# Reordering the row loads, crossbar transposes and value loads of each batch in a fused attention and feed-forward kernel

## Chip, cores, metric

One core of a Trainium2 chip. The metric is the time of the whole program on the device in microseconds (us); quoted times are medians of all runs of a kernel. Runs marked slow, more than 1.5% above the fastest of the same kernel, are left out of ratios. A ratio is the mean time of one kernel's fast runs over the mean of the other's of the same rounds on the same chip, so it is not quite the ratio of the medians.

## The reference

Attention over a band of 16 positions on each side plus block summaries (maximum of 32 keys, mean of 32 values), then a feed-forward layer with a scaled swish.

```python
# q, k, v: (4 batches, 8 heads, 768, 64) float32;  w_in (512, 2048), w_out (2048, 512)
k_sum = k.reshape(B, H, 24, 32, D).max(axis=3)
v_sum = v.reshape(B, H, 24, 32, D).mean(axis=3)
scores_l = scale * q @ k.T ;  masked to |i - j| < 16
scores_s = scale * q @ k_sum.T + log(32)
a = softmax(concat(scores_l, scores_s))
x = a @ concat(v, v_sum)                    # then (B*S, 512)
h = x @ w_in
out = (h * sigmoid(beta * h)) @ w_out       # (3072, 512) float32
```

## The kernel before

Eight blocks of 384 rows (4 batches, 2 halves each) are worked through. Block i has an h phase (16 tiles of `x @ w_in`, Silu) and an o phase (`@ w_out`); beside the o phase PE also makes the scores and the attention of block i+1. Side work is put at numbered positions of the two phases: `side_h`, position p, stands ahead of h tile p; `side_o`, position p, stands ahead of o part p (12 parts of 4 matmuls). Each engine's instructions are issued in the order in which they are written.

Three kinds of transfer serve the next batch. GpSimd (POOL) issues loads that change float32 to bf16: key rows, query rows, and values in two halves ("even" and "odd" tiles). SP issues crossbar transposes of the loaded key rows (`k_bar`, four a batch), of query rows (`q_bar`, one a block) and of half of the attention result x (`x_dma`, one a block), and the stores of the output. `hold(src)` is a one-element copy on POOL: nothing behind it on POOL is issued before `src` is there.

```python
def k_bar(b, g):                                        # SP
    nc.sync.dma_start_transpose(out=kT_bufs[i][:, W:W + S]..., in_=krow[(b, g // 2)]...)
def q_bar(b, c):                                        # SP
    nc.sync.dma_start_transpose(out=t..., in_=qrow.pop((b, c))...)
def x_dma(b, g, c):                                     # SP
    nc.sync.dma_start_transpose(out=x_tile(b, c)[:, g:g + 2]..., in_=xp[(b, g // 2, c)]...)
def q_fill(b, g, c): ...                                # DVE: qTT -> q2, two copies a pair
def hold(src):                                          # POOL
    nc.gpsimd.tensor_copy(out=tick[:], in_=src)
# ... in block i = (b, c):
        elif b + 1 < B:
            hold(xT[(b, c)][0:1, npair - 1, 0:1])
            if c == 0:
                for g in PAIRS:
                    load_k_rows(b + 1, g)
                load_q_rows(b + 1, 0)
                load_v6(b + 1)
                load_v_even(b + 1)
            else:
                load_v_odd(b + 1)
                load_q_rows(b + 1, 1)
# ...
            elif c == 0:
                    for g in PAIRS:
                        add(side_o, 7 + g, k_bar, b + 1, g)
# ...
            if nxt > 2:
                add(side_h, 0, q_bar, b2, c2)           # (b2, c2): the next block
                for g in PAIRS:
                    add(side_h, 10 + g, q_fill, b2, g, c2)
            for g in PAIRS:
                add(side_o, (-1, 0, 3, 4)[g], scores, b2, g, c2)
# ...           # x of the next block: pairs 0 and 1 by x_dma at side_o 5.1,
                # pairs 2 and 3 on PE (x_pe) at side_o 9
```

The softmax here doesn't subtract the row's maximum and nothing guards it: scores larger than these inputs give would overflow.

## Time and profile before

| | before |
|---|---|
| time, median of 2 runs | 246.98 us (246.56 to 247.40) |
| span of the profiled run | 243.7 us |
| PE busy | 223.5 us (92%) |
| mean granted PE clock | 0.97 |

PE (the matmul engine, TensorE) sets the pace, so the table is read for what it lacks: 20 us in which PE stands still, and some time in which it is busy at a lower clock. (The granted clock is the share of its full clock that PE was given, as the trace records it.) Which lines show where that is comes with the prediction below.

### The profile page before, as it was taken

To read this page: it belongs to the slowest core of one execution; us is meant where nothing else is said; L and a number is where in the kernel's file an instruction comes from. 1 tells how busy PE (TensorE), PEld (TensorE's weight loads), DVE (VectorE), ACT (ScalarE), POOL (GpSimd) and SP (SyncE) were. 2 spreads that over 40 slices of the span, in tenths; PEclk is the share of its full clock that TensorE was granted. 3 is DMA by queue.
4 is the path that set the end of the run, shared out by engine and by line. 5 is a ranking of instruction groups with operands and counts; after the bars stand their busy time and mean duration, and the time that the engine had idled before them with its cause. 6 is when DMAs were issued, how large, how long until landed. Compare 5 with 4: busy or idle time off the path is not lost.

```text
span 243.7 us, 4675 instructions
## 1 busy us (share of the span) xinstructions
PE 223.5 (92%) x1871; PEld 122.0 (50%) x1871; DVE 118.5 (49%) x337; ACT 152.4 (63%) x246; POOL 68.3 (28%) x106
## 2 busy tenths in 40 slices
PE   6969799979999999999769999999669999999993
PEld 2544456445555565555335555555334456556541
DVE  7564797958945504635386504634384613520000
ACT  2766379537767489648735489657725389939610
POOL 7649491560000396034000396044000000000000
PEclk9997999999999999999979999999968999999999
DMA  7999999999701399999931299999931340121012
GB/s 129 181 179 178 203 195 193 200 146 167 119 0 46 78 167 137 145 189 124 172 20 46 76 168 138 159 175 130 165 19 45 79 108 3 43 78 43 0 43 86
DMA packets 100565, 27.86 MB, mean 114 GB/s; under 512 B 89392, under 2 KB 97600, under 8 KB 100544
## 3 DMA queue, kind: packets, MB, share of 16 engines
q0 software_dynamic: 71664, 14.98, 77.6%
q1 hardware_dynamic: 28736, 12.46, 25.0%
q8 instruction: 14, 0.23, 0.4%
q10 hardware_dynamic: 144, 0.13, 0.2%
q14 instruction: 7, 0.06, 0.1%
HBM read 31.52 MB, written 6.29 MB: 155 GB/s over the span
## 4 chain that ended last, share of the span: by engine, by line
PE 68%; DMA 14%; DVE 8%; ACT 5%; issue 2%; POOL 1%; SPq 0%; ACTq 0%; DVEq 0%; POOLq 0%
PE o_ps L472 33%; PE h_ps L454 23%; DMA qTT<-qrow 13%; PE s_ps L329 4%; PE av_ps L355 3%; DMA qnat<-in_q_dram 2%; DVE w_out_sb L442 2%; DVE q L271 1%; PE px L372 1%; DVE v L397 1%; PE vm_ps L390 1%; ACT h_sb L462 1%; DVE x_nat L359 1%; DVE km L239 1%; DVE q L298 1%
## 5 line engine op out<-in xcount | busy, mean ns | idle before, releaser
L472 PE MATMUL o_ps<-w_out_sb,h_sb 128*128 128x512 bf16 x384 | 94.5, 389 | 0.0
L454 PE MATMUL h_ps<-xT,w_in_sb 128*128 128x384 bf16 x512 | 86.7, 326 | 1.1 <-ACT h_sb L462 0.8
L462 ACT ACTIVATE h_sb<-h_ps,beta_sb 128x384 bf16<-128x384 f32 x128 | 73.9, 581 | 18.6 <-PE h_ps L454 11.1
L454 PEld LDWEIGHTS <-w_in_sb 128*128 128x128 bf16 x512 | 49.2, 98 | 35.5 <-issue 3.0
L472 PEld LDWEIGHTS <-h_sb 128*128 128x128 bf16 x384 | 35.7, 100 | 35.9 <-issue 3.6
L331 ACT ACTIVATE attn<-s_ps 128x768 bf16<-128x768 f32 x28 | 22.2, 811 | 14.8 <-PE s_ps L329 14.7
L271 DVE COPY q<-qTT 64x384 bf16<-64x384 bf16 x40 | 13.9, 347 | 35.4 <-DMA qTT<-qrow 34.8
L484 ACT COPY o_sb<-o_ps 128x512 f32<-128x512 f32 x23 | 13.5, 586 | 27.5 <-PE o_ps L472 24.9
L334 DVE TENSOR_TENSOR attn<-attn,mask 128x768 bf16<-128x768 bf16 x28 | 15.5, 558 | 21.8 <-ACT attn L331 21.1
L490 POOL COPY tick<-xT 1x1 bf16<-1x1 bf16 x4 | 0.7, 178 | 76.2 <-ACT xT L373 76.2
L329 PE MATMUL s_ps<-q,kw 128*128 128x128 bf16 x168 | 14.5, 231 | 8.2 <-DVE q L271 8.1
L329 PEld LDWEIGHTS <-kw 128*128 128x128 bf16 x168 | 12.2, 103 | 13.3 <-issue 9.3
L359 DVE TENSOR_TENSOR x_nat<-av_ps,r 128x384 bf16<-128x384 f32 x32 | 17.8, 558 | 1.1
L257 DVE TENSOR_REDUCE km<-kT 128x24 bf16<-128x768 bf16 x8 | 7.6, 950 | 17.7 <-DMA kT<-krow 17.7
L373 ACT COPY xT<-px 128x384 bf16<-128x384 bf16 x19 | 9.1, 479 | 10.7 <-PE px L372 10.5
L100 POOL DMA_DIRECT2D qrow<-in_q_dram x15 | 13.4, 914 | 2.0 <-DMA krow<-in_k_dram 2.0
L95 POOL DMA_DIRECT2D krow<-in_k_dram x16 | 13.1, 852 | 0.9 <-issue 0.9
L355 PEld LDWEIGHTS <-attn 128*64 128x64 bf16 x384 | 8.0, 111 | 9.5 <-issue 5.5
L397 DVE COPY v<-vm 32x1536 bf16<-32x1536 bf16 (+1 forms) x20 | 10.9, 558 | 3.6 <-ACT vm L393 2.7
L479 DVE COPY o_sb<-o_ps 128x256 f32<-128x256 f32 x1 | 0.4, 424 | 24.3 <-PE o_ps L472 24.3
L157 ACT ACT_TABLE_LOAD x9 | 11.5, 1283 | 0.9 <-PEq L705 0.8
L247 DVE COPY kw<-kT 128x288 bf16<-128x288 bf16 x56 | 12.0, 268 | 0.0
(96 smaller groups left out, 182.3 us busy)
## 6 DMA issues: line engine op xcount, KB each, us to landing
out_dram<-o_sb SPq DMA_DIRECT2D x23, 256.0 KB, 3.0
v<-in_v_dram POOLq DMA_DIRECT2D x3, 768.0 KB, 10.4
w_in_sb<-in_moe_w_in_dram POOLq DMA_DIRECT2D x4, 512.0 KB, 6.8
w_out_sb<-in_moe_w_out_dram POOLq DMA_DIRECT2D x4, 512.0 KB, 15.9
qrow<-in_q_dram POOLq DMA_DIRECT2D x15, 128.0 KB, 11.8
krow<-in_k_dram POOLq DMA_DIRECT2D x16, 96.0 KB, 6.7
vs<-in_v_dram SPq DMA_DIRECT2D x3, 384.0 KB, 6.2
v<-in_v_dram POOLq DMA_DIRECT2D x2, 576.0 KB, 12.7
```

The costliest lines, as they stand in the source:

```text
L100: nc.gpsimd.dma_start(out=qrow[(b, c)][:, m], in_=q_r2[b, c, :, m])
L271: nc.vector.tensor_copy(out=q2[r, :, hh].rearrange("p (m t) f -> p m t f", t=2), in_=t[r])
L329: nc.tensor.matmul(big[:, j // 3, j % 3 * P:(j % 3 + 1) * P], kw[:, j, :], q2[:, j].rearrange("p h q -> p (h q)"), start=True, stop=True)
L331: nc.scalar.activation(out=a.rearrange("p (k n) -> p k n", k=2), in_=big[:, :, 0:CT], func=ACTF.Exp, scale=scale)
L334: nc.vector.tensor_mul(out=av4, in0=av4, in1=mask[:, c * TC:(c + 1) * TC, None, :].to_broadcast([P, TC, 2, QT]))
L355: nc.tensor.matmul(ov[r, j // 2, hh], av4[:, j, hh], vr[:, hh, c * TC + j, 0:D + 1], start=True, stop=True)
L359: nc.vector.tensor_mul(out=x, in0=ov[:, :, :, 0:D], in1=r[:, :, :, None].to_broadcast([P, CC, 2, D]))
L397: nc.vector.tensor_copy(out=v_rows(b, g)[KR:P, :, t0:t1, 0:D], in_=vm[KR:P, 2 * i:2 * i + 2, None].to_broadcast([P - KR, 2, t1 - t0, D]))
L454: nc.tensor.matmul(h_ps[(i, ni)][:, 0:CT], w_in_sb[:, ki, ni * P:(ni + 1) * P], x[:, ki], start=(ki == 0), stop=(ki == k1 - 1))
L462: nc.scalar.activation(out=h_sb[i][:, ni], in_=hp[:, 0:CT], func=ACTF.Silu, scale=beta_sb[:, ni:ni + 1])
L472: nc.tensor.matmul(o_ps[ms][:], h_sb[i][:, ni, ms * P:(ms + 1) * P], w_out_sb[:, ni, :], start=(ni == 0), stop=(ni == k2 - 1))
L484: nc.scalar.copy(out=o_sb[:], in_=o_ps[ms][:])
```

## The change

Its intent: bring a new batch's keys and queries first, transpose them as they land (in the h phase, where PE needs nothing from the SP queue), and let the values come only after the last key transpose.

```diff
         elif b + 1 < B:
-            hold(xT[(b, c)][0:1, npair - 1, 0:1])
             if c == 0:
+                hold(xT[(b, c)][0:1, npair - 1, 0:1])
                 for g in PAIRS:
                     load_k_rows(b + 1, g)
                 load_q_rows(b + 1, 0)
                 load_v6(b + 1)
-                load_v_even(b + 1)
             else:
-                load_v_odd(b + 1)
                 load_q_rows(b + 1, 1)
 ...
                     for g in PAIRS:
-                        add(side_o, 7 + g, k_bar, b + 1, g)
+                        add(side_h, 14, k_bar, b + 1, g)
+                    add(side_h, 14, q_bar, b + 1, 0)
+
+                    def v_next(b=b):
+                        hold(kT_bufs[(b + 1) % 2 * npair + npair - 1][0:1, W:W + 1])
+                        load_v_even(b + 1)
+                        load_v_odd(b + 1)
+
+                    add(side_h, 14, v_next)
 ...
-                at_v = 13.5 if i == 1 else 10
+                at_v = 14
 ...
-                add(side_h, at_v, vsum)
+                if i == 1:
+                    add(side_o, 0.5, vsum)
+                else:
+                    add(side_h, at_v, vsum)
                 for g in PAIRS:
-                    add(side_h, at_v + 1 + g, ... v_spread ...)
+                    add(side_o, 1 + g * .5, ... v_spread ...)
             if nxt > 2:
-                add(side_h, 0, q_bar, b2, c2)
 ...
+            if c and b + 1 < B:
+                add(side_o, 8.5, q_bar, *divmod(i + 2, NC))
 ...
             def v1():
-                hold(w_out_sb[0:1, k2 * 3 // 4 - 1, 0:1])
+                hold(w_out_sb[0:1, k2 - 1, 0:1])
 ...
-            add(side_o, 3.2, v1)
+            add(side_o, 5.7, v1)
```

## The prediction

> **What bounds the kernel now.** I read the page's first parts, then cut the span into stages, then the waits of each stage, then the order of time around the waits. Eight blocks of rows are worked through; a stage here is one block's h phase (64 matmuls of w_in, with Silu) followed by its o phase (48 matmuls of w_out, with the scores and the attention of the next block).
>
> ```profile
> PE 223.5 (92%) x1871; PEld 122.0 (50%) x1871; DVE 118.5 (49%) x337; ACT 152.4 (63%) x246; POOL 68.3 (28%) x106
> PE 68%; DMA 14%; DVE 8%; ACT 5%; issue 2%; POOL 1%; SPq 0%; ACTq 0%; DVEq 0%; POOLq 0%
> ```
>
> PE is busy 92% of 243.7 us, so a gain comes only from its 20.2 us of idle and from time in which it is busy at a lower clock. The DMA share of the chain is no 14% to win: the chain runs back through the query transpose while PE works beside it. What counts is how late that transpose ends. The stages tell it (columns: stretch, length, then busy us and instructions of PE, PEld, DVE, ACT, POOL, then granted clock, DMA share, GB/s):
>
> ```profile
> 83.90:107.80 23.90, 23.82 (x192) 13.44 (x190) 7.75 (x20) 17.83 (x28) 11.98 (x15) 1.00 1.95 154
> 107.80:138.90 31.10, 27.19 (x200) 14.74 (x198) 17.99 (x53) 17.93 (x28) 4.95 (x6) 0.95 0.93 92
> 138.90:162.50 23.60, 23.60 (x192) 13.37 (x190) 7.75 (x20) 17.82 (x28) 12.01 (x15) 1.00 1.85 157
> 162.50:195.30 32.80, 28.61 (x199) 15.00 (x198) 17.79 (x53) 17.93 (x28) 4.79 (x5) 0.90 0.88 87
> 195.30:218.90 23.60, 23.60 (x192) 13.39 (x190) 7.75 (x20) 17.82 (x28) 0.00 (x0) 1.00 0.23 60
> ```
>
> These are blocks 2 to 6. Blocks 2, 4 and 6 take 23.6 to 23.9 us with no PE idle. Blocks 3 and 5, which prepare a new batch, take 31.1 and 32.8 at clocks of 0.95 and 0.90. Their waits (first block 3, then block 5; the columns are us in total, times, longest):
>
> ```profile
> PE s_ps L329 <- DVE q L271: 3.9, 2, 3.4
> DVE q L271 <- DMA qTT<-qrow: 3.5, 1, 3.5
> ```
> ```profile
> PE s_ps L329 <- DVE q L271: 4.2, 2, 3.7
> DVE q L271 <- DMA qTT<-qrow: 2.9, 1, 2.9
> ```
>
> So PE stands still because the new batch's queries reach it late. In block 5, second by second, the clock is seen to fall after that:
>
> ```profile
> 177.00:178.00 1.00, 0.00 (x0) 0.00 (x0) 0.36 (x2) 0.00 (x0) 0.00 (x0) 1.00 1.17 71
> 178.00:179.00 1.00, 0.62 (x6) 0.61 (x6) 0.95 (x3) 0.00 (x0) 0.00 (x0) 0.54 0.00 0
> 183.00:184.00 1.00, 1.00 (x4) 0.29 (x2) 0.91 (x2) 0.00 (x0) 0.00 (x0) 0.50 0.00 0
> 185.00:186.00 1.00, 1.00 (x11) 0.65 (x10) 0.00 (x0) 0.30 (x1) 0.00 (x0) 1.00 0.00 0
> ```
>
> Why are the queries late? On the SP queue (in order), the four key transposes of batch 2 stand behind block 2's output store and x transpose; the first goes out at 103.97, and the query transpose behind them at 111.26. By then the odd half of the values (issued at 107.71) and the next query rows (from 109.48) are in flight too, and it lands 11.5 us later, at 122.8. The five query transposes landed in 8.1, 11.5, 7.7, 11.4 and, the last one, with no loads beside it, 3.7 us.
>
> A second, smaller site is block 0's o phase. The row is start, length, what:
>
> ```profile
> 47.21 3.06 DVE L442 TENSOR_SCALAR w_out_sb<-w_out_sb,inv_beta 128x512 bf16<-128x512 bf16 x4
> 51.03 0.34 PE L372 MATMUL px<-identity,x_nat 128*128 128x128 bf16 x3 [1.60 <-DVE x_nat L359]
> ```
>
> Four scalings of w_out take 3.06 us here, while four took 1.14 from 44.18; the longest is 1,627 ns where the median of all sixteen is 347. At that time POOL is issuing the value loads of batch 1 (45.88 to 49.9), and PE then waits 1.60 us for x_nat, which stands behind the scalings.
>
> **What the Trainium skill says.** First, "TensorE: Matmul & The Clock Gate", section "Part 1: The HAM clock gate": the array drops to half clock after about one idle window of 3.4 us, and needs about 3.4 us of sustained work to come back. The trace agrees: waits whose longest pieces are 3.4 and 3.7 us are followed by clocks of 0.50, for about 3.5 us in block 3 (123.4 to 126.9) and 7 us in block 5 (177.9 to 184.9). Second, "SBUF — State Buffer", section "Who interferes with whom": a tensor_scalar in a two-port mode and a GpSimd operation exclude one another for a whole instruction, and the descriptors of DMAs issued from GpSimd are written through that port. The 1,627 ns beside POOL's issues fits; the trace shows the coincidence, not the port. Third, "DMA: Bandwidth & Descriptors", section "Queues, rings and completion order": each DMA engine goes round its queues packet by packet, so a transpose on the SP queue shares with loads on the GpSimd queue. The 3.7 us alone against 11.5 beside loads agrees.
>
> **The change part by part.** PE's instruction count does not change (3,743 rows in both orders); DVE's 40 query copies, 8 maxima and 56 key copies stay, as do all loads and transposes. It is an exchange of order.
>
> (a) Block 2 (and 4): the four key transposes and the first query transpose go ahead of the o phase's store and x transpose on SP, so they go as the rows land. The key loads are issued from 83.65 to 90.1, and landed in 3.0 to 7.4 us (median 6.7). Each key transpose occupies the engines about 1.25 us (four landed between about 104.5 and 109.5), and slows the loads it cuts into. I estimate the last key transpose lands at 96 to 98, the query rows at 96 to 98, and the query transpose, beside the value load, 8 us later: 104 to 106, in place of 122.8. The queries are first needed in block 3 near 118, so the wait goes, with 12 us to spare.
>
> (b) The values are held until that last key transpose: even half issued near 97 instead of 94.6, odd half behind it instead of at 107.7. At the 10.4 and 12.7 us to landing of these loads, shortened for the odd half because it follows in one queue, I expect 108 to 110 and 114 to 117. The value sum on PE moves to h tile 14 of block 3 (about 117), the attention matmuls that read the odd half come at about 128. Both hold.
>
> (c) The second query transpose (for the batch's second half) moves from the start of the even block to the o phase before it, before the key loads. It ends near 86 instead of 93.5; it cost PE 0.08 us, so this wins nothing by itself, but it leaves the engines free for the key loads.
>
> (d) Block 1's value sum and spreads move into its o phase. PE work is the same 1.63 us (1.41 + 0.22); the spreads (1.97 us DVE) sit before attention, where DVE waited for ACT 1.44 and 0.50 us anyway. About 0.
>
> (e) Block 0: value loads wait for the last scaling. DVE saves 3.06 − 1.14 = 1.92 us; PE waits 1.60 of it. Take 1.6. The loads move some 3 us later, and the value sum that needs them moves later too.
>
> The sum: block 3 without waits should be an even block plus its value sum, 23.6 + 1.63 = 25.2 us. Gain 31.1 − 25.2 = 5.9 in block 3, 32.8 − 25.2 = 7.6 in block 5. This holds the pure stall (3.9 and 4.2) and the half-clock time (1.5 and 3.3: half of 3.0 and 6.5 busy us at 0.50, which adds to 5.4 and 7.5, so the two counts agree). With (e): 5.9 + 7.6 + 1.6 = 15.1 us. Against this I put 1 us for each of the two batches for the rival below: 247.0 − 15.1 + 2.0 = 233.9, called 234.
>
> **The rivals.** First: the wait moves to the x transpose. Before, it was issued at 102.64 and landed in 3.7 us, at 106.3, and block 3's first h matmul ran at 107.89, so it has 1.5 us of slack. Afterwards it stands on SP behind a query transpose that runs beside both halves of the values and the next query rows, with no pause at 104.5 to 110 as now. SP was held 3.8 us by one such transpose. If SP is held until 103, or the x transpose takes 8 us like its larger relative, block 3 starts 1 to 4 us late. Against it: at 102.64 the even values were in flight too, and it took 3.7. A wait under 3.4 us should not cost the clock, so this would take back 2 to 6 us in all: 236 to 239. I give it 30%, and 1 us a batch on average.
>
> Second: the total of transfers binds. Then something merely comes late elsewhere, at (b). Before, DMA worked from 83.6 to about 123 of a 55 us cycle (two stages) with a hole near 110, so there is room; if the odd values came after 128, up to 3 us a batch would come back: 237 to 240. 7%.
>
> Third: the transpose lateness is hidden and the stall has another cause, such as DVE's work before the query copies. DVE sat idle 3.5 us just before the first of them, so I give it 3%; the time would be about 245.
>
> Fourth: the clock does not recover because some new short waits add up to an idle window. Then 3 to 5 us of the gain are lost: 237 to 239. 7%.
>
> **Range and chances.** With no rival, 231.9 to 232.5; with a small x wait, 234; with the first rival at full strength, 238. So 230.5 to 238.5 for 8 in 10. The threshold for faster by 2% is 242.0, which needs 5 of the 15 us; only the third rival, or two others together, miss it. Faster 0.95, same 0.04, slower 0.01.
>
> **What would show it.** Right: in blocks 3 and 5 the wait of scores for the query copies is under 0.3 us, the granted clock is 1.00, and both stages take 25 to 26 us; key transposes lie between 87 and 98; the scalings are all near 350 ns and PE's 1.60 us wait is gone. Wrong at (a) or the first rival: PE waits for the x transpose at the start of blocks 3 and 5. Wrong at (b): the value sum or the attention waits for a value load. It would be wrong altogether if the key transposes, beside their own loads, took so long that the hold kept the values past 117.

## The result

| | before | after |
|---|---|---|
| time, median of 2 runs | 246.98 us | 237.03 us (236.59 to 237.48) |
| ratio of fast runs | | 0.9597 (95%: 0.9492 to 0.9703) |
| span of the profiled run | 243.7 us | 235.8 us |
| mean granted PE clock | 0.97 | 0.985 |

Two later groups on other chips gave the changed kernel a ratio of 0.9582 and of 0.9645. It is faster by 3.6 to 4.2%; its medians in the three groups (237.03, 236.39 and 238.50 us) lie 2.4 to 4.5 us above the 234 us that I had said.

From the page of the kernel before, the chain of work that ended last; then the page of the changed kernel. In the chain, the query transpose (qTT) has gone and the x transpose (xT) has come:

```profile
PE o_ps L472 33%; PE h_ps L454 23%; DMA qTT<-qrow 13%; PE s_ps L329 4%; PE av_ps L355 3%; DMA qnat<-in_q_dram 2%; DVE w_out_sb L442 2%; DVE q L271 1%; PE px L372 1%; DVE v L397 1%; PE vm_ps L390 1%; ACT h_sb L462 1%; DVE x_nat L359 1%; DVE km L239 1%; DVE q L298 1%
```
```profile
PE 221.7 (94%) x1871; PEld 121.2 (51%) x1871; DVE 116.7 (50%) x337; ACT 152.0 (64%) x246; POOL 67.9 (29%) x106
PE h_ps L454 36%; PE o_ps L472 32%; DMA xT<-x_nat 5%; PE s_ps L329 4%; PE av_ps L355 4%; PE vm_ps L390 3%; DMA qnat<-in_q_dram 2%; PE px L372 1%; PE vm_ps L166 1%; DVE km L239 1%; POOL knat L81 1%; DVE q L298 1%; ACT q L298 1%; POOL qnat L8
```

The stages of blocks 2 to 6 of the changed kernel, with the columns of the same table in the prediction:

```profile
83.12:106.94 23.82, 23.81 (x191) 13.29 (x189) 11.17 (x29) 17.80 (x28) 15.53 (x18) 1.00 1.74 148
106.94:134.02 27.08, 25.44 (x197) 13.91 (x198) 14.34 (x45) 17.81 (x28) 1.10 (x3) 1.00 1.17 113
134.02:157.85 23.83, 23.82 (x191) 13.29 (x189) 11.17 (x27) 17.80 (x28) 14.96 (x17) 1.00 1.53 147
157.85:187.18 29.33, 27.13 (x198) 14.51 (x199) 15.23 (x48) 17.80 (x28) 1.95 (x3) 0.94 1.26 101
187.18:210.83 23.65, 23.65 (x192) 13.38 (x191) 7.74 (x20) 17.80 (x28) 0.00 (x0) 1.00 0.21 54
```

Blocks 3 and 5 went from 31.1 and 32.8 us to 27.1 and 29.3; an even block plus its value sum would be 25.2. What holds them now is at their start. The timeline of PE, with the wait and its releaser in brackets:

```profile
108.58 9.27 PE L454 MATMUL h_ps<-xT,w_in_sb 128*128 128x384 bf16 x56 [1.64 <-DMA xT<-x_nat]
160.05 10.95 PE L454 MATMUL h_ps<-xT,w_in_sb 128*128 128x384 bf16 x56 [2.21 <-DMA xT<-x_nat]
```

The wait for the queries is gone, and a wait for x has come. The same 56 matmuls take 9.27 us in block 3 and 10.95 in block 5, and the windows of block 5, microsecond by microsecond, say why: the granted clock (third column from the end) falls after the wait.

```profile
159.00:160.00 1.00, 0.00 (x0) 0.00 (x0) 1.00 (x5) 0.00 (x0) 0.80 (x1) 1.00 2.29 166
161.00:162.00 1.00, 1.00 (x5) 0.50 (x4) 0.95 (x5) 0.58 (x1) 0.00 (x0) 0.50 2.42 155
164.00:165.00 1.00, 1.00 (x8) 0.59 (x7) 0.00 (x0) 0.73 (x2) 0.00 (x0) 1.00 2.47 158
```

Around block 2's x transpose the SP queue stands like this (start, length of the issue, what), with the query transpose and a store shortly ahead of x; the key transposes, not shown, were issued from 87.33 to 95.1:

```profile
99.88 1.27 SPq L262 DMA_TRANSPOSE qTT<-qrow  x1
101.25 0.98 SPq L485 DMA_DIRECT2D out_dram<-o_sb  x1
102.33 1.26 SPq L378 DMA_TRANSPOSE xT<-x_nat  x1
```

and POOL lets the values go just then, when the last key transpose has landed:

```profile
100.44 0.18 POOL L490 COPY tick<-kT 1x1 bf16<-1x1 bf16 x1 [7.94 <-DMA kT<-krow]
100.96 2.23 POOL L414 DMA_DIRECT2D v<-in_v_dram  x1 [0.34 <-issue]
```

x landed 6.2 us after its issue in block 2 and 6.5 in block 4 (3.7 and 3.0 before).

In block 0 the scalings are quick again (DVE's timeline), and PE's wait of 1.60 us became 0.57 us, now for a copy on ACT:

```profile
47.39 1.13 DVE L442 TENSOR_SCALAR w_out_sb<-w_out_sb,inv_beta 128x512 bf16<-128x512 bf16 x4
```

From the first scores matmul of block 0's o phase to the end of the last wait (59.43 before, 58.55 after) it takes 19.4 us where it took 20.4. Block 1, to which part (d) belongs, takes 24.57 us in both.

### The profile page after: what moved, and what is told of

Its sections match the earlier page's. It is cut to its first block, busy times and chain, and to the rows that moved or that the text cites. A ratio compares the mean times of both kernels' runs of the same rounds, so it can differ in the third digit from the quotient of the medians.

```text
span 235.8 us, 4672 instructions
## 1 busy us (share of the span) xinstructions
PE 221.7 (94%) x1871; PEld 121.2 (51%) x1871; DVE 116.7 (50%) x337; ACT 152.0 (64%) x246; POOL 67.9 (29%) x106
## 3 DMA queue, kind: packets, MB, share of 16 engines
q1 hardware_dynamic: 28736, 12.46, 25.2%
## 4 chain that ended last, share of the span: by engine, by line
PE 82%; DMA 7%; DVE 3%; ACT 2%; POOL 2%; issue 1%; DVEq 0%; POOLq 0%
PE h_ps L454 36%; PE o_ps L472 32%; DMA xT<-x_nat 5%; PE s_ps L329 4%; PE av_ps L355 4%; PE vm_ps L390 3%; DMA qnat<-in_q_dram 2%; PE px L372 1%; PE vm_ps L166 1%; DVE km L239 1%; POOL knat L81 1%; DVE q L298 1%; ACT q L298 1%; POOL qnat L84 1%; DVE v L397 0%
## 5 line engine op out<-in xcount | busy, mean ns | idle before, releaser
L454 PE MATMUL h_ps<-xT,w_in_sb 128*128 128x384 bf16 x512 | 88.3, 330 | 4.9 <-DMA xT<-x_nat 3.9
L472 PE MATMUL o_ps<-w_out_sb,h_sb 128*128 128x512 bf16 x384 | 91.7, 379 | 0.0
L454 PEld LDWEIGHTS <-w_in_sb 128*128 128x128 bf16 x512 | 49.7, 99 | 40.6 <-DMA xT<-x_nat 4.8
L472 PEld LDWEIGHTS <-h_sb 128*128 128x128 bf16 x384 | 34.7, 98 | 34.0 <-issue 0.4
L484 ACT COPY o_sb<-o_ps 128x512 f32<-128x512 f32 x23 | 13.4, 585 | 27.6 <-PE o_ps L472 25.0
L247 DVE COPY kw<-kT 128x288 bf16<-128x288 bf16 x56 | 14.1, 331 | 0.0
L100 POOL DMA_DIRECT2D qrow<-in_q_dram x15 | 13.4, 934 | 0.0
L329 PEld LDWEIGHTS <-kw 128*128 128x128 bf16 x168 | 11.1, 98 | 4.2
L329 PE MATMUL s_ps<-q,kw 128*128 128x128 bf16 x168 | 12.8, 219 | 0.0
L355 PE MATMUL av_ps<-v,attn 128*64 128x65 bf16 x384 | 10.1, 199 | 1.2 <-DVE v L397 1.1
```

The source lines that it names most:

```text
L100: nc.gpsimd.dma_start(out=qrow[(b, c)][:, m], in_=q_r2[b, c, :, m])
L247: nc.vector.tensor_copy(out=kw[:, t::2, 0:KR], in_=src)
L329: nc.tensor.matmul(big[:, j // 3, j % 3 * P:(j % 3 + 1) * P], kw[:, j, :], q2[:, j].rearrange("p h q -> p (h q)"), start=True, stop=True)
L355: nc.tensor.matmul(ov[r, j // 2, hh], av4[:, j, hh], vr[:, hh, c * TC + j, 0:D + 1], start=True, stop=True)
L454: nc.tensor.matmul(h_ps[(i, ni)][:, 0:CT], w_in_sb[:, ki, ni * P:(ni + 1) * P], x[:, ki], start=(ki == 0), stop=(ki == k1 - 1))
L472: nc.tensor.matmul(o_ps[ms][:], h_sb[i][:, ni, ms * P:(ms + 1) * P], w_out_sb[:, ni, :], start=(ni == 0), stop=(ni == k2 - 1))
```

## The experiments

The edits are against the changed kernel, but for the two that start from the kernel before. The table is the overview; ratios are to the kernel before in the same rounds.

| run | edit | median us | ratio (95%) | PE waits for x, blocks 3 and 5, us |
|---|---|---|---|---|
| after_again | none | 236.39 | 0.9582 (0.949 to 0.967) | 2.19, 2.06 |
| x_on_pe | x of blocks 2, 4 on PE | 232.36 | 0.9456 (0.939 to 0.952) | none |
| x_before_q | x ahead of the query transpose | 232.21 | 0.9442 (0.939 to 0.950) | none |
| v_after_x | values held until x | 231.38 | 0.9429 (0.935 to 0.950) | none |
| keep_busy | dummy matmuls in the wait | 236.59 | 0.9599 (0.954 to 0.965) | 0.41, 0.91 behind 1.73 of dummies |
| only_late_v1 | before, part (e) alone | 244.88 | 0.9904 (0.984 to 0.997) | none |
| only_k_early | before, early transposes alone | 251.17 | 1.0147 (1.007 to 1.022) | 7.39, 7.66 |
| v_not_held | no hold on the values | 248.83 | 1.0095 (1.004 to 1.015) | 6.34, 6.58 |
| not_held_x_first | no hold, x first | 243.75 | 0.9993 (0.990 to 1.009) | 3.33, 3.40 |
| q_late_again | part (c) undone | 233.69 | 0.9572 (0.948 to 0.966) | 1.12, none |
| after_pair | none | 238.50 | 0.9645 (0.958 to 0.971) | 2.20, 3.32 |
| q_late_pair | part (c) undone | 234.50 | 0.9507 (0.945 to 0.956) | 0.90, 1.44 |

Groups on one chip: the first four; the next four; the next two; the last two. The profiled runs of only_late_v1, only_k_early and after_pair were slow: their waits are given, but not compared in size with those of fast runs.

### Is x the missing time?

The yardstick of the group:

> The changed kernel unaltered, as the yardstick for the others of this group. Both theories: 236 to 238 us, PE waits for the x transpose of about 1.6 and 2.2 us at the start of blocks 3 and 5, and about 3.5 us of half clock after the second of these.

It came out at 236.39 us, and in its trace it was block 3 that lost the clock (56 matmuls in 10.96 us after a wait of 2.19) and not block 5 (9.27 after 2.06).

> The changed kernel, but in blocks 2 and 4 the first two x tiles are transposed on PE as the other two are, so that nothing of x goes through the SP queue there. Theory (what my sum missed is the x transpose landing late, and the half clock that follows): the 3.9 us of wait and about 1.7 us of half clock go, 12 transposes on PE of 0.17/3 us each add 0.7 us: 232 us. Rival (the remaining time comes from the transfers in total, which then stop something else, such as the value sum or the attention): 235 to 237 us, with a new PE wait for a value load.

```diff
-                if g < 2 and i:
+                if g < 2 and i and not (c == 0 and b + 1 < B):
                     if g:
                         add(side_o, 5.1, x_dma, b2, 0, c2)
+                elif g < 2 and i:
+                    add(side_o, 8 + g * .1, x_pe, b2, g, c2, act_copy, "s", 2)
```

232.36 us: as the theory had it to half a microsecond, and no new wait for a value load. What was missing to the 231.9 us of my sum without a rival is x and its consequences.

### What makes x late: the queue ahead of it, or the loads beside it?

> The changed kernel, but the first query transpose of the new batch is issued on SP after the x transpose of blocks 2 and 4 instead of ahead of it. Theory A (x is late because a query transpose and a 256 KB store stand ahead of it in the queue): x lands 3.7 us or less after its issue, the wait at blocks 3 and 5 goes, 232 to 233.5 us, and the query transpose, now beside the value loads, lands later but before 118. Theory B (x is late because of the value loads beside it): x still takes about 6 us and the time stays at 236 to 238 us.

```diff
-                    add(side_h, 14, q_bar, b + 1, 0)
+                    add(side_o, 5.2, q_bar, b + 1, 0)
```

232.21 us, x landed 2.8 us after its issue: what theory A says. But the transfers, microsecond by microsecond, show that x's packets passed from 103 to 104 (723 of them) and the values' first ones at 104 to 105, so this run does not refute B. The query transpose, now beside the values, took 10.5 us in one block and 6.4 in the other, and PE waited for neither; it waited 0.65 us for a value load in block 3.

> The changed kernel, but the value loads wait for the x transpose of the same block instead of for the last key transpose, and the value sum of blocks 3 and 5 is put behind the first quarter of the o phase, since the loads come some 5 us later. Theory B (value loads beside x make it late): x lands in about 4 us, wait gone, 232 to 234 us unless the values themselves now come late, in which case PE waits for them at the value sum. Theory A (the queue ahead): x still lands near 6 us after issue, the waits of 1.6 and 2.2 us stay, 236 to 238 us.

```diff
-                        hold(kT_bufs[(b + 1) % 2 * npair + npair - 1][0:1, W:W + 1])
+                        hold(xT[(b, 1)][0:1, 1, 0:1])
                         load_v_even(b + 1)
                         load_v_odd(b + 1)
-                    add(side_h, 14, v_next)
+                    add(side_o, 5.3, v_next)
 ...
-                if i == 1:
-                    add(side_o, 0.5, vsum)
-                else:
-                    add(side_h, at_v, vsum)
+                add(side_o, 0.5, vsum)
```

231.38 us, the fastest of all. The query transpose and a store stand ahead of x as before, and x lands after 2.8 and 3.1 us. So the queue ahead is not enough to make x late, against A, and with the value loads out of the way x is on time, as B has it. (The value sum, moved as well, stands behind the matmuls that wait for x, so it is not what brought x early.) The changed kernel's own transfers agree: from 103.5 to 106 SP's queue moved 811 packets, which is nearly all of x's 768 and the end of a store; from 106 to 107 POOL's loads moved 1,172 packets and SP's queue none, only then came 30 last ones of SP's queue, and x landed at 108.5. Blocks 3 and 5 of this run:

```profile
106.61:132.00 25.39, 25.13 (x196) 13.90 (x197) 16.10 (x48) 17.82 (x28) 5.24 (x7) 1.00 1.41 120
155.65:181.04 25.39, 25.12 (x196) 13.90 (x198) 15.24 (x46) 17.82 (x28) 6.12 (x6) 1.00 1.53 116
```

That is, but for 0.2 us, the 25.2 us which the prediction took for a block without waits.

The next run was meant to separate the two from the other side. It takes the hold away and puts x ahead of the query transpose, so that x should have only a store ahead and running loads beside:

> Both changes of the runs before together: the values not held, and the first query transpose behind the x transpose on SP. The loads are then in flight from 93 to about 118, and x, issued near 102, has only a 256 KB store ahead of it. Theory A (what is ahead in the queue makes x late): x lands in 2.8 to 3.7 us, no wait, 232 to 234 us. Theory B (a transpose beside running loads gets one packet for one of theirs, or fewer, whatever is ahead of it): its 768 packets, at some 400 a us and with the 4 us of near standstill that the run without the hold showed, take 5 to 8 us: PE waits of 1 to 3 us at blocks 3 and 5, 236 to 242 us.

```diff
-                        hold(kT_bufs[(b + 1) % 2 * npair + npair - 1][0:1, W:W + 1])
 ...
-                    add(side_h, 14, q_bar, b + 1, 0)
+                    add(side_o, 5.2, q_bar, b + 1, 0)
```

x took 8.7 and 8.8 us and PE waited 3.3 and 3.4 us, as theory B has it. But x did not have only the store ahead: the last key transpose, issued at 95.88, took 9.2 us beside the loads, to 105.1, and x was issued at 102.71. From 104 to 107 SP's queue moved 161 packets, of which the store's 128 (of 2 KB) fill most, beside 2,590 of the loads; x's own began at about 107. So this run alone does not rule out the queue ahead as a part of the 8.7 us; it shows that what stands ahead is itself slowed by the loads. That the loads are needed to make x late is shown by v_after_x. The time, 243.75 us, lies 1.75 above the range of the expectation, as the half clock after the waits, which I had left out, cost some 1.6 us in each of the two blocks (56 matmuls in 10.83 and 10.95 us).

### Is the hold on the values needed?

> The changed kernel without the hold on the values: both halves are issued straight behind the row loads. Theory (hold needed): the key and query transposes run beside the values, x is later still than in the changed kernel (PE waits of 4 us or more), 239 to 244 us. Rival (hold worth nothing): 235 to 238 us as the changed kernel.

```diff
-                        hold(kT_bufs[(b + 1) % 2 * npair + npair - 1][0:1, W:W + 1])
                         load_v_even(b + 1)
                         load_v_odd(b + 1)
```

248.83 us: 0.9% slower than the kernel before (a ratio of 1.0095, with an interval above 1), and beyond the 244 us that I had allowed. The hold alone is worth about 12 us (5% by the ratios, from runs on different chips), more than the whole change gained. PE's timeline:

```profile
113.69 11.92 PE L454 MATMUL h_ps<-xT,w_in_sb 128*128 128x384 bf16 x56 [6.34 <-DMA xT<-x_nat]
172.18 11.69 PE L454 MATMUL h_ps<-xT,w_in_sb 128*128 128x384 bf16 x56 [6.58 <-DMA xT<-x_nat]
```

The transfers of this run (queue: packets, MB, share of 16 engines' time), first the microsecond from 104 to 105, when the query transpose had been issued for 4 us, then that from 107 to 108; q0 carries POOL's loads, q1 SP's transposes and stores:

```profile
q0 software_dynamic: 1053, 0.13, 400.6%
q1 hardware_dynamic: 3, 0.00, 0.6%
```
```profile
q1 hardware_dynamic: 414, 0.11, 79.7%
q0 software_dynamic: 415, 0.05, 79.6%
```

From 101 to 105 the loads moved about 1,100 packets a us and SP's queue 8; from 106 to 109 they went one for one. Here a transpose beside such loads first hardly moved, then got half of the packets.

> The kernel before with the key transposes and the first query transpose of a new batch in the h phase, but the value loads where they were (even half straight behind the row loads, odd half after the x of the even block), the value sum where it was, and part (e) left out. Theory (the hold on the values is needed, since the even half would run beside the transposes): the last key transpose and the query transpose land some 5 us later than in the changed kernel, x of the even block stands behind them on the queue, and PE waits 4 us or more for x at the start of blocks 3 and 5, with half clock after it: 242 to 246 us. Rival (the order on the SP queue alone does it and the hold is worth nothing): 237 to 239 us, 1.5 us above the changed kernel for part (e).

The kernel before with `k_bar` and the batch's first `q_bar` at `side_h` 14 and everything else as it was:

```diff
-                        add(side_o, 7 + g, k_bar, b + 1, g)
+                        add(side_h, 14, k_bar, b + 1, g)
+                    add(side_h, 14, q_bar, b + 1, 0)
 ...
-                add(side_h, 0, q_bar, b2, c2)
+                if c == 0:
+                    add(side_h, 0, q_bar, b2, c2)
```

251.17 us, worse than expected (242 to 246) and slower than the kernel before, by 0.7 to 2.2%. The order on SP that looks like the heart of the change costs 1.5% by itself; of the runs here it wins only together with the hold.

### Part (e), the scalings

> The kernel before with part (e) of the change alone: the value loads of batch 1 wait for the last scaling of w_out instead of the twelfth. Theory: the four slow scalings (3.06 us) go back to 1.14 us, the PE wait of 1.60 us for x_nat falls to under 0.6, and the time falls by 1.0 to 1.6 us to about 245.5; blocks 3 and 5 stay as before. Rival (the scalings are slow for another reason, or the delay of the loads costs as much later): no change of the scalings, or the same time within 0.3 us.

```diff
-                hold(w_out_sb[0:1, k2 * 3 // 4 - 1, 0:1])
+                hold(w_out_sb[0:1, k2 - 1, 0:1])
-            add(side_o, 3.2, v1)
+            add(side_o, 5.7, v1)
```

The longest scaling fell from 1,627 to 378 ns, and the wait for x_nat is gone (0.57 us for ACT remain); such single durations at one spot are read from the slow trace. The ratio of 0.9904 is 2.4 us by the means, with an interval of 0.8 to 3.9 us (the interval's ends times 246.8); the trace of the changed kernel shows 1.05 us. Expected were 1.0 to 1.6, which the interval holds. No cost of the later loads shows.

### The clock after a wait

> The changed kernel with 8 dummy matmuls of 512 columns (8 x 0.216 = 1.7 us at full clock) put on PE ahead of the h phase of blocks 3 and 5, where it waits 1.6 to 2.2 us for x. Theory (a wait of about 2.2 us is enough to let the clock fall to half, now and then, for some 3.5 us, which costs 1.7 us): both h phases run at clock 1.00, their 56 matmuls take 9.3 us in both, and no run is of the slow kind: about 235 us with a smaller spread. Rival (the half clock is a matter of the chip and not of the idle time): one of the two blocks still takes 10.9 us for the 56 matmuls and the time stays at 236 to 238 us.

```diff
+        if c == 1 and i > 1 and b + 1 < B:
+            keep = ps.tile([P, 512], f32, name="keep", tag="t", bufs=1)
+            blanks(keep[:], 8)
```

In the one trace, both blocks ran their 56 matmuls in 9.26 us at full clock, as the theory says, but the time, 236.59 us, is that of the changed kernel: x itself landed about 0.4 us later in this trace, and the runs of both scatter over 2 us. One trace without a fall does not show that the dummies prevented it. Inconclusive.

The kept traces say more about when the clock falls. PE's lines of after_again, a fast run, and of after_pair, a slow one:

```profile
108.74 10.96 PE L454 MATMUL h_ps<-xT,w_in_sb 128*128 128x384 bf16 x56 [2.19 <-DMA xT<-x_nat]
161.75 9.27 PE L454 MATMUL h_ps<-xT,w_in_sb 128*128 128x384 bf16 x56 [2.06 <-DMA xT<-x_nat]
```
```profile
110.26 10.96 PE L454 MATMUL h_ps<-xT,w_in_sb 128*128 128x384 bf16 x56 [2.20 <-DMA xT<-x_nat]
164.52 9.28 PE L454 MATMUL h_ps<-xT,w_in_sb 128*128 128x384 bf16 x56 [3.32 <-DMA xT<-x_nat]
```

The spells of half clock last 3.41 us (the changed kernel's from 160.52 to 163.93) or twice that, and two spells of one trace begin a whole multiple of 3.41 us apart: 123.46 and 178.07 in the kernel before (16 times 3.413), 112.27 and 170.29 in v_not_held (17 times). This fits a clock that is judged once in each window of 3.41 us, in fixed step. The waits of 2.19, 2.20 and 2.21 us each lay whole inside the window before the fall (in the changed kernel 157.84 to 160.05 in 157.11 to 160.52). Counted on from the fall in the same trace, the edge of a window cut the wait of 2.06 us into 1.15 and 0.91 (at 160.84) and that of 3.32 into 1.30 and 2.02 (at 162.50), and the clock stayed. So in these blocks a window with 2.2 us of idle cost the clock and one with 2.0 did not: where a wait lies in the window counts, and not its length alone. By the same count the waits of keep_busy, with the dummies taken as idle, would have been cut too (at 109.04 and 160.24, counted back from the half clock that begins at 235.33, after PE's last work), so that run could hardly have shown a fall. At the kernel's start some falls follow windows with less idle time; those were not taken apart.

### Part (c), the second query transpose

> The changed kernel with part (c) undone: the second query transpose of a batch goes back to the start of the even block, where it runs beside the key loads. Theory (c frees the engines for the key loads and transposes): the key transposes stand behind it on SP and start at 90 in place of 87, everything behind them, to x, comes some 2 us later, PE waits of 3 to 5 us for x: 239 to 243 us. Rival (c wins nothing, as there is slack): 235.5 to 237.5 us as the changed kernel.

```diff
-            if c and b + 1 < B:
-                add(side_o, 8.5, q_bar, *divmod(i + 2, NC))
 ...
             if nxt > 2:
+                if c == 0:
+                    add(side_h, 0, q_bar, b2, c2)
```

A miss: 233.69 us where I expected 239 to 243. On that chip the kernel before was quicker too, and the ratio, 0.9572, was that of the changed kernel elsewhere, so both were run again side by side:

> The changed kernel again, on one chip with the next run, since the run with part (c) undone came out at 233.7 us on a chip of its own, where the kernel before was 0.7 us faster too. 235 to 237 us, PE waits for x of 1.6 to 2.2 us in both blocks.

> Part (c) undone, beside the changed kernel. Theory (new: the later query transpose delays the last key transpose, with it the hold and so the value loads, so that x gets through ahead of them; part (c) loses by this what it wins): the waits for x together under 2.5 us in place of 4, the time 1 to 2.5 us under the changed kernel of the same chip. Rival (the 233.7 us were the chip): within 0.7 us of it.

238.50 us (above the 235 to 237 expected) and 234.50 us, ratios 0.9645 and 0.9507, with intervals that do not touch. By the means of the fast runs (237.3 and 233.9) undoing (c) wins 3.4 us, more than the 1 to 2.5 expected. (The first comparison, on two chips, showed none of it: 0.9572 against 0.9582.) The waits of PE for x (us in total, times, longest), first in the fast trace of the changed kernel, then in that of q_late_pair:

```profile
PE h_ps L454 <- DMA xT<-x_nat: 3.9, 2, 2.2
```
```profile
PE h_ps L454 <- DMA xT<-x_nat: 2.3, 2, 1.4
```

With (c) undone, the query transpose is issued at 84.36 and runs beside the key loads; the last key transpose lands later, and the hold lets the values go 19.7 us after the start of block 2 in place of 17.3 (102.65 − 83.00 against 100.44 − 83.12), that is 1.1 us ahead of x's issue in place of 1.9. The values come later, and more of x is through before them. That fits what v_after_x shows. The traces hold 1.6 us less of waits (3.9 against 2.3) and one fall of the clock less (1.7 us), 3.3 in all; that the later values are the whole reason is argued, not shown.

## Why the prediction was right, and where it was off

- **The bound and the wait** were right. The query wait (3.9 and 4.2 us) is gone; blocks 3 and 5 hold what was lost (PE does the same 1,871 matmuls and 1,871 weight loads before and after; the prediction's 3,743 is one more than the two pages have), and without waits they take 25.39 us (v_after_x) where I had 25.2. The sum without a rival, 231.9 us, is met by x_on_pe (232.36).
- **(a), early transposes:** right in kind, about 3 us too early in the estimates. I had the last key transpose landed at 96 to 98; the hold saw it at 100.44, and the query transpose was issued at 99.88. I had counted 1.25 us for each key transpose, from four that I took to land between 104.5 and 109.5 in the kernel before. That was misread: they landed at 108.6, 109.7, 110.7 and, the last one, beside the odd values, at 117.2 (2.8 to 8.0 us after issue). In the changed kernel, beside the row loads, it was 5.5 to 9.0 us. The first query transpose landed at 103.6, just ahead of the 104 to 106 that I had given, but by luck: it went out later than I thought, and then took 3.7 us and not 8, as the hold kept the values away from it.
- **(b), the values:** later than I had them (the even half issued at 100.96 for "near 97", and landed 13.4 us later, at 114.4, for 108 to 110; the odd half at about 119 for 114 to 117), and still in time, as said: PE waited for no value at the sum. I had not seen that the hold is worth 12 us, since I thought of transposes and loads as sharing throughout.
- **(c):** said to win nothing by itself and to help the key loads. It cost 3.4 us in the paired runs.
- **(d):** about 0 expected, 24.57 us in both.
- **(e):** 1.6 us expected, 1.05 found within the trace; a copy on ACT bounds the spot at 0.57 us.
- **The step that failed** is the size of the first rival: 1 us a batch. Its sign, which the prediction named (PE waits for the x transpose at the start of blocks 3 and 5), came in both batches (1.6 and 2.2 us), where I gave it 30%, and with the half clock it took 1.9 us from block 3 and 4.1 from block 5 (27.1 and 29.3 against 25.2), 6.0 in all in place of 2.0. The rival's own range, 236 to 239 us, was right. With 1.05 in place of 1.6 for (e) the sum would be 238.5 us; measured were 237.03, 236.39 and 238.50.
- **The argument against that rival** failed as well. I took x's 3.7 us in the kernel before as landing beside the values; its transfers show the values running out just then: 1,092 packets of the loads from 102 to 103, 247 in the next microsecond, 20 in the one after. x had run into a gap.
- **"A wait under 3.4 us should not cost the clock"** was wrong: in the fast traces waits of 2.19 and 2.21 us did, 1.7 us each (10.96 and 10.95 in place of 9.27), while 1.64 and 2.06 did not; in the slow trace of after_pair 2.20 did and 3.32 did not (10.96 and 9.28). The place of a wait in the windows of 3.41 us tells them apart. So of the fourth rival, a clock lost to new waits, a part came: one fall of 1.7 us in each trace of the changed kernel, but from one wait of 2.2 us and not from several short ones.
- **Second and third rivals** did not come: no wait for the values at the sum or the attention of blocks 3 and 5, and DVE was not the cause, as the wait for its query copies went with the earlier transpose.

## What to carry to other kernels

When a late transfer is moved ahead in a queue, ask what now stands behind it and which loads run beside that: here the wait went from the queries to x, and without the hold it would have been worse than before. A transfer that a busy engine waits for belongs in a gap between bulk loads, and the simplest way to make one is to hold the next load until that transfer has landed, not until some other has: this gave 231.4 us, 2.1% under the changed kernel (231.38 against 236.39 on one chip). Putting x first on the queue (232.21) or on PE (232.36) did as much within the noise. Before taking a landing time as "beside a load", look whether that load's packets still flow.

## What the Trainium skill lacked or had wrong

- "TensorE: Matmul & The Clock Gate", section "HAM oscillation — how this bites in real kernels": its rule is that PE should have no idle gaps over about 3.4 us. As a safe limit it fails here: each of three waits of 2.19 to 2.21 us was followed by half clock, which cost 1.7 us, while one of 3.32 us was not (two of these four in a slow run). The page calls the window free-running, and the spacing of the spells agrees; but a window of which 2.2 us of 3.4 were idle was enough.
- "DMA: Bandwidth & Descriptors", section "Queues, rings and completion order": the round of packets between queues is there, 414 to 415 in one microsecond. It lacks what came before it: about 4 us in which SP's queue moved some 8 packets a us beside 1,100 of POOL's loads. No run here shows the reason.
- No page that I read has what a crossbar transpose costs beside loads issued by POOL: x took 2.8 us without, and 8.7 to 10.9 in the midst of them, with what stood ahead of it on SP slowed as well.
